# Two attention-plus-FFN layers on one core: the last FFN weights issued from ScalarE's queue instead of SyncE's

## The chip, the core and the metric

The kernel runs on one core of a Trainium2 chip. The metric is the device time of one execution in microseconds (us). The kernel before takes 2695.49 us, the median of three runs between 2694.4 and 2696.01 us. Lower is better.

## What is computed

The reference is two identical layers, each a recurrent attention followed by a gated feed-forward network (FFN). Cut to what matters:

```python
for s in range(n_seg):                      # 64 segments of 32 tokens, one after the other
    h = concat([mem, x[:, s*32:(s+1)*32]])  # 8 memory rows + 32 tokens
    q, k, v = h @ Wq, h @ Wk, h @ Wv        # 32 heads of 128, model width 576
    p = softmax(mask(q k^T * 128**-0.5))
    o = (p v) @ Wo
    mem = o[:, :8]                          # the next segment needs this segment's output
    outs.append(o[:, 8:])
x = x + outs(layernorm(x))
x = x + (silu(layernorm(x) @ w1) * (layernorm(x) @ w3)) @ w2     # FFN width 4608
# the same two lines once more (the second layer, same weights)
```

The memory rows make the segments a chain: segment s+1 cannot start before segment s has its output. The FFN has no such chain.

## The kernel before

**Steps and jobs.** Both layers run interleaved. `step(t)` does segment t of layer 0 and segment t - 8 of layer 1 together, so that there are 72 steps; the last eight serve layer 1 alone. After every fourth step comes `job(j)`, the FFN for a block of 128 tokens of each layer. An FFN job runs over 18 slices of 256 of the 4608 columns; a slice needs the tile `W13` (slices of w1 and w3, 256 KB twice and 32 KB twice) and `W2C` (288 KB in all of w2, two slices to a "down" product). These tiles have two buffers each and are loaded again for each job. The last job has no steps left beside it.

**Weights that stay, and the tail loads.** Wq and Wk lie in the tile `W`, Wv in `WV`, Wo in `WO`, for the whole kernel. When the last step has read a part of Wq and Wk for the last time, those columns are free, and the last job's FFN weights are put there: `tail_load(i, what)` (L705) for i = 0 to 3. With `what` = 0 it loads w1 and w3 for four slices into 1024 columns of `W`, in four transfers of 1024, 1024, 128 and 128 KB; with `what` = 1 it loads w2 for the same slices into `WV`, in one transfer of 1152 KB. All eight calls make 20 transfers, 14.2 MB. The last two of the 18 slices are kept from the job before. L477 holds what a call waits for: part i of `W` waits for the last step's Q and K projections numbered 2i and 2i+1 of eight (QK and QKt in the code), the parts of `WV` for the last step's V product. In the profile `W13` and `W` both appear as `W`, since buffer numbers are left out; their transfers are told apart by size.

**The last step.** Its four groups of eight heads each go through: projections (`HT,W` products), their copies out of PSUM (`QKT`), scores (`QKT` products), exponential on ScalarE (`SME<-SME`, one for each group, so four), row sums and probabilities on VectorE (`STAT`, `PB`), a transpose (`ident,PB`), its copies (`PTS`), the product with V (`PTS,V`), its copies (`OT`), and the product with Wo (`OT,WO`). Pieces of the FFN job before stand between them as filler: `XTB,W` products, a tanh on ScalarE (`HTT<-bank`), two multiplications on VectorE, and the down product `W2C,HTT`. After the last step a layer norm follows, and then the last job's 18 slices.

**What sets the order.** The order of TensorE's work is a string written out by hand (`ORDER`, L199 to L222; Q and q are projections, S scores, T transpose, P product with V, O product with Wo, F and f FFN). `plan()` (L76) lays everything else around it: a greedy list scheduler over queues ACT (ScalarE), DVE (VectorE), POOL, DMA (the queue that SyncE issues) and SWD. It picks by estimated times (`dur`, `lat`) and due times (`prio`), and gives copies marked "AD" to ScalarE or VectorE, whichever is free first by its estimate. It also hands out the eight PSUM banks. The order that it finds on each engine is then fixed: instructions of one engine are emitted in that order. `Emitter.dma` (L599) issues a transfer from SyncE's queue, `Emitter.adma` (L602) from ScalarE's queue; the latter is used only four times in the kernel before, at the very start.

**Completion semaphores.** The framework below the kernel adds the waits. Transfers from both hardware queues share eight completion semaphores, handed out in turn, in the order in which the plan emits the transfers. So each of them waits, at its place in its engine's queue, for the transfer that used its semaphore before to land, in most places the one eight earlier.

Of the kernel before, what the change touches and what calls it, by code (L numbers as in the profile page):

```python
# [9 lines left out]
ACT = mybir.ActivationFunctionType  # L10
# [3 lines left out]
P = 128  # L14
R64 = 64
D = 576
# [159 lines left out]
def actc(*ns):  # L176

    return sum(max(0.067 + n * 0.000833, 0.19) for n in ns)


def dve(*ns):
    return sum(max(0.065 + n / 960.0, 0.19) for n in ns)
# [11 lines left out]
def ewh(*ns):  # L194
    return (actc(*ns), dveh(*ns))
# [36 lines left out]
def make_nodes(em, nseg, pools, o=Opt, dma_bw=230e3, load_bw=400e3):  # L232
# [4 lines left out]
    def node(*a, **k):  # L237
        n = Node(*a, **k)
        nodes.append(n)
        return n  # L240

    def banks(n=2):
        return [Slot("bank") for _ in range(n)]

    nst = nseg + LAG
    kb = lambda rows, cols: rows * cols * 2
# [9 lines left out]
    def load(name, nbytes, prio, fn, deps=()):  # L256
        return node("DMA", nbytes / load_bw, fn, deps=deps, prio=prio, name=name, lat=2.0)
# [8 lines left out]
    b = banks(1)  # L266
# [10 lines left out]
    def ln_nodes(tag, src, xn, deps, prio, writes, warm=False):  # L277

        a = node("DVE", 1.16, em.ln_stats(src, xn), deps=deps, prio=prio, acq=[] if src is xn else [xn], name=tag + "stats")
        p_ = node("POOL", 0.45, em.ln_pow(xn), deps=[a], prio=prio, name=tag + "pow")  # L280
        c = node("DVE", 0.46 if src is xn else 0.66, em.ln_norm(src, xn), deps=[p_], prio=prio, name=tag + "norm")
        b = Slot("bank", users=len(writes))
        d = node("PE", 5 * 0.056, em.ln_tr(xn, b, warm), deps=[c], prio=prio, mode="full/col", acq=[b], rel=[xn], name=tag + "tr")
        out = []
        for wr, cost, more in writes:
            out.append(node("AD", cost, wr(b), deps=[d] + more + out[-1:], prio=prio, rel=[b], name=tag + "wr"))
        return out
# [12 lines left out]
    def ht_set(li, g, nodes_):  # L300
        i = -1
        for j in range(4):
            t = 4 * g + j + LAG * li
            i += j == 0 or role(t) == 0
            ht_ready[li, t] = nodes_[i]
# [136 lines left out]
    def post(li, g):  # L442

        b = banks(1)
        prio = 4 * g + 4 + LAG * li
        d = node("PE", 5 * 0.056, em.post_tr(li, g, b[0]), deps=[d for j in range(4) for d in yx[li, 4 * g + j]] + ([xr_ld[g]] if li == 0 else []),
                 prio=prio, mode="full/col", acq=b, name="POST")
        return node("DVE", dve(576), em.post_add(li, g, xr[g], b[0]), deps=[d], prio=prio, rel=b, name="POSTa")
# [5 lines left out]
    def job(j):  # L454

        ents = [(0, j)] if 0 <= j < ngrp else []
        if 0 <= j - 2 < ngrp:
            ents.append((1, j - 2))
        if not ents:
            return  # L460
        s0 = 4 * j + 4 if j < ngrp else 4 * j - 4 + LAG
        ne = len(ents)
        last = s0 >= nst
        wr = []
        prev_ff = list(last_up)
        cost = ewh(640)
        for (bi, g) in reversed(ents):
            pa = post(bi, g)
            wr += ln_nodes("F", xr[g], Slot("xn"), [pa], s0, [((lambda bi: lambda b: em.xtb_write(bi, b))(bi), cost, prev_ff)], last)
        mm = (128 * ne / 2.4 + 2.5) / 1000  # L470
        w2_last = {}
        tail = None
        if last:
            v_done, qk_done = last_reads
            tail = []
            for i in range(4):
                parts = [(0, 9 * 1024, qk_done[4 * i:4 * i + 4]), (1, 8 * 576, v_done)]  # L477
                tail += [[load("tail", kb(128, c), s0 + o.tail_at + 0.01 * i, em.tail_load(i, what), deps=dep) for what, c, dep in parts]] * 2

        npp = NPR // 2  # L480
        for at, pp in enumerate([npp - 1] + list(range(npp - 1)) if last else range(npp)):
            mids, w2s, htts, lds = [], [], [], []
            stays = last and pp == npp - 1
            for pr_ in (2 * pp, 2 * pp + 1):
                prio = s0 + o.ff + (o.win if s0 + 4 < nst else o.last_win) * (2 * at + pr_ % 2) / NPR
                if stays:
                    w13, w2 = kept[pr_]
                    ld = []
                    w2s.append(w2)
                elif last:  # L490
                    w13 = w2 = None
                    ld = tail[pp]
                else:
                    keep = s0 < nst <= s0 + 4 and pp == npp - 1
                    w13, w2 = Slot("w13", users=2 + keep), Slot("w2", users=ne + keep)
                    kept[pr_] = w13, w2
                    ld = [node("DMA", kb(1152, 256) / dma_bw, em.load_w13(pr_, w13), prio=prio - 1, acq=[w13], lat=2.0, name="W13")]
                    lds.append(node("DMA", kb(256, 576) / dma_bw, em.load_w2(pr_, w2), prio=prio - 0.99, acq=[w2], lat=2.0, name="W2l"))
                    w2s.append(w2)
                b = banks()  # L500
                htt = Slot("htt", users=ne)
                rel13 = [w13] if w13 else []
                fm = node("PE", 16 * mm, em.ffn_up(ents, pr_, w13, b, last and not stays, False), deps=wr + ld, prio=prio, mode="full/col",
                          acq=b + [htt], rel=rel13, name="FF")
                ff = node("PE", 2 * mm, em.ffn_up(ents, pr_, w13, b, last and not stays, True), deps=wr + ld, prio=prio + o.fft, mode="row",
                          acq=b + [htt], rel=rel13, name="FFt")
                a = node("ACT", actc(256 * ne), em.ffn_tanh(ents, b, htt), deps=[fm, ff], prio=prio - 0.5, name="tanh")
                c = node("DVE", 2 * dve(256 * ne) + 0.13, em.ffn_mul(ents, b, htt), deps=[a], prio=prio - 0.5, rel=b, name="mul")
                last_up[:] = [fm, ff]
                mids.append(c)  # L510
                htts.append(htt)
            for (bi, g) in ents:
                b = banks()
                d = node("PE", 8 * 0.1225, em.ffn_down(bi, pp, htts, w2s, b, last and not stays), deps=mids + lds, prio=prio + o.w2,
                         mode="full/col", acq=b, rel=htts + w2s, name="W2b" if bi else "W2")
                es = [node("DVE", dve(288), em.ffn_add(g, h, xr[g], b[h]), deps=[d], prio=prio + o.w2, rel=[b[h]], name="W2a")
                      for h in (0, 1)]
                w2_last[bi] = es
        for (bi, g) in ents:
            if bi == 0:  # L520
                ht_set(1, g, ln_nodes("L1", xr[g], Slot("xn"), w2_last[0], s0 + LAG - 4.2, ht_writes(1, g)))
            else:
                xn = Slot("xn")
                c = node("ACT", actc(576), em.fin_cast(xr[g], xn), deps=w2_last[1], prio=s0 + LAG - 4.2, acq=[xn], rel=[xr[g]], name="fin")
                node("SWD", 1.0, em.store(g, xn, last), deps=[c], prio=s0 + LAG - 4.2, rel=[xn], lat=3.0, name="store")
# [42 lines left out]
class Emitter:  # L568
# [136 lines left out]
    def tail_load(self, i, what):  # L705

        def f(n):
            T = self.T
            fa = i * 1024
            t13, t2 = T.W[:, :, fa:fa + 1024], T.WV[:, i * 8 * D:(i + 1) * 8 * D].rearrange("p (b d) -> p b d", b=8)  # L710
            if what != 1:
                for kind, wd in ((0, self.a.w1), (1, self.a.w3)):
                    self.dma(t13[:, 4 * kind:4 * kind + 4], wd[0:4 * P, fa:fa + 1024].rearrange("(c p) f -> p c f", p=P))
                for kind, wd in ((0, self.a.w1), (1, self.a.w3)):
                    self.dma(t13[kind * R64:(kind + 1) * R64, 8], wd[4 * P:D, fa:fa + 1024])
            if what != 0:
                self.dma(t2, self.a.w2[fa:fa + 1024, :].rearrange("(b p) d -> p b d", p=P))
            for h in range(4):
                self.tail_w[4 * i + h] = (t13[:, :, h * 2 * P:(h + 1) * 2 * P], t2[:, 2 * h:2 * h + 2])
        return f  # L720
# [607 lines left out]
```

## Time and profile before

| | before |
|---|---|
| time, median of 3 | 2695.49 us |
| span of the profiled run | 2694.7 us |
| PE busy | 2622.5 us (97%) |
| PEld (weight loads) busy | 2286.7 us (85%) |
| DVE busy | 2103.0 us (78%) |
| ACT busy | 1361.9 us (51%) |
| data moved | 322.08 MB, mean 120 GB/s |
| start of the last step's first projection | 2621.18 us |
| last tail transfer issued | 2673.23 us |

The table is from the page and the timeline. Over the whole span TensorE is nearly always busy, but the change concerns only the end: the last step starts at 2621 us, and everything that the change moves happens after it. So the views to read are those of the last 75 us: what each engine did there in order of time, what the SyncE queue waited for, and what the DMA engines moved. Busy time does not count DMA-issuing instructions; they stand in the timeline as SPq or ACTq.

### The profile page before, as it was taken

How to read it: one execution, taken by the hardware profiler on the slowest of the kernel's cores; microseconds unless marked ns; L12 is line 12 of the kernel's file. 1: busy time of each engine (PE TensorE's matmuls, PEld its weight loads, DVE VectorE, ACT ScalarE, POOL GpSimd, SP SyncE). 2: the span in 40 equal slices, each digit the busy share in tenths (PEclk: the TensorE clock that was granted, in tenths of full speed). 3: DMA queues.
4: the chain of work that ended last, by engine and by line, in shares of the span. 5: the costliest groups of instructions: out<-in, count | busy, mean ns of one | idle time of the engine just before them, and what ended most of it. 6: DMA issues, size and time to landing. Idle time of an engine off the chain costs nothing.

```text
span 2694.7 us, 137011 instructions
## 1 busy us (share of the span) xinstructions
PE 2622.5 (97%) x60931; PEld 2286.7 (85%) x60995; DVE 2103.0 (78%) x5463; ACT 1361.9 (51%) x3938; POOL 332.5 (12%) x400
## 2 busy tenths in 40 slices
PE   5999999999999999999999999999999999999998
PEld 4788888889888888888888888888888888888886
DVE  5777886887888788787878878787887878787876
ACT  2655554554545455454545445454545545454542
POOL 1111110110111011011101101010110101011110
PEclk8999999999999999999999999999999999999999
DMA  9064524343342334334233433423243442434457
GB/s 317 4 178 115 156 85 129 89 128 109 109 127 80 109 97 128 109 114 127 78 111 91 128 108 117 126 80 116 83 128 108 117 126 66 121 89 135 128 168 246
DMA packets 478178, 322.08 MB, mean 120 GB/s; under 512 B 26024, under 2 KB 467760, under 8 KB 476944
## 3 DMA queue, kind: packets, MB, share of 16 engines
q1 hardware_dynamic: 474048, 305.43, 38.4%
q8 instruction: 477, 7.82, 1.2%
q0 software_dynamic: 3024, 6.93, 0.9%
q10 hardware_dynamic: 512, 0.94, 0.2%
q14 instruction: 117, 0.96, 0.1%
HBM read 308.49 MB, written 2.36 MB: 115 GB/s over the span
## 4 chain that ended last, share of the span: by engine, by line
PE 85%; DVE 7%; DMA 3%; ACT 2%; issue 1%; SPq 1%; POOL 0%; ACTq 0%; DVEq 0%
PE bank L591 85%; DVE STAT L597 1%; ACT V L594 1%; DVE SME L597 1%; DVE HTT L597 1%; SPq L600 1%; DMA W<-in_B_w_dram 1%; DVE PB L597 1%; DMA W<-in_A_Wk_dram 1%; DVE V L597 1%; DVE XN L597 0%; DMA WO<-in_A_Wo_dram 0%; DVE LNS L597 0%; DMA XN<-in_A_x_dram 0%; ACT PTS L594 0%
## 5 line engine op out<-in xcount | busy, mean ns | idle before, releaser
L591 PEld LDWEIGHTS <-W 128*128 128x128 bf16 (+2 forms) x32176 | 1267.8, 100 | 130.0 <-issue 62.6
L591 PE MATMUL bank<-HT,W 128*128 128x80 bf16 (+3 forms) x23040 | 811.9, 197 | 21.6 <-issue 9.4
L591 PE MATMUL bank<-XTB,W 128*64 128x256 bf16 (+5 forms) x9136 | 659.3, 263 | 5.6 <-DMA W<-in_B_w_dram 3.7
L594 ACT ACTIVATE QKT<-bank 128x64 bf16<-128x64 f32 (+2 forms) x1500 | 349.7, 312 | 352.7 <-PE bank L591 347.1
L1006 POOL MEMSET PB<- 128x1024 bf16 x288 | 274.1, 952 | 1831.6 <-PE bank L591 1532.6
L591 PE MATMUL bank<-OT,WO 128*128 128x80 bf16 (+3 forms) x11520 | 407.0, 198 | 3.8 <-ACT OT L594 1.3
L591 PEld LDWEIGHTS <-WO 128*128 128x128 bf16 (+1 forms) x11520 | 379.9, 102 | 21.2 <-issue 9.0
L594 ACT ACTIVATE V<-bank 64x512 bf16<-64x512 f32 (+1 forms) x606 | 343.0, 585 | 94.7 <-PE bank L591 86.1
L591 PE MATMUL bank<-WV,HT 128*32 128x512 bf16 (+4 forms) x3520 | 364.5, 382 | 6.6 <-issue 3.8
L591 PE MATMUL bank<-W2C,HTT 128*64 128x288 bf16 (+1 forms) x3072 | 323.6, 287 | 1.4 <-DMA W2C<-in_B_w_dram 1.0
L597 DVE TENSOR_REDUCE STAT<-SME 104x8 f32<-104x320 f32 (+1 forms) x576 | 274.2, 476 | 11.4 <-ACT SME L594 6.1
L594 ACT ACTIVATE HTT<-bank 128x512 bf16<-128x512 f32 (+1 forms) x324 | 176.6, 553 | 208.5 <-PE bank L591 207.5
L597 DVE TENSOR_TENSOR PB<-SME,STAT 40x128 bf16<-40x128 f32 (+4 forms) x912 | 275.0, 336 | 8.5 <-DVE STAT L597 0.5
L597 DVE SCALAR_TENSOR_TENSOR XR<-bank,XR 128x288 f32<-128x288 f32 x576 | 245.9, 446 | 25.0 <-PE bank L591 20.8
L591 PEld LDWEIGHTS <-HT 128*32 128x32 bf16 (+5 forms) x3584 | 154.2, 98 | 124.8 <-issue 17.4
L597 DVE SCALAR_TENSOR_TENSOR HTT<-HTT,bank 128x512 bf16<-128x512 bf16 (+1 forms) x324 | 201.8, 623 | 74.2 <-ACT HTT L594 69.9
L591 PEld LDWEIGHTS <-HTT 128*64 128x64 bf16 (+1 forms) x3136 | 223.7, 105 | 35.7 <-issue 2.4
L594 ACT ACTIVATE OT<-bank 128x320 bf16<-128x320 f32 (+1 forms) x420 | 155.2, 403 | 147.6 <-PE bank L591 144.6
L597 DVE TENSOR_TENSOR HTT<-HTT,bank 128x512 bf16<-128x512 bf16 (+1 forms) x324 | 203.6, 629 | 27.7 <-DVE HTT L597 0.5
L594 ACT ACTIVATE SME<-SME 104x320 f32<-104x320 f32 (+1 forms) x288 | 135.2, 470 | 166.8 <-DVE SME L597 165.1
L597 DVE CAST QKT<-bank 128x128 bf16<-128x128 f32 (+4 forms) x548 | 147.6, 316 | 87.9 <-PE bank L591 85.6
L594 ACT ACTIVATE PTS<-bank 128x320 bf16<-128x320 f32 (+1 forms) x383 | 143.9, 403 | 131.6 <-PE bank L591 118.4
(61 smaller groups left out, 1831.3 us busy)
## 6 DMA issues: line engine op xcount, KB each, us to landing
W<-in_B_w_dram SPq DMA_DIRECT2D x612, 256.0 KB, 3.5
W2C<-in_B_w_dram SPq DMA_DIRECT2D x306, 288.0 KB, 3.2
W<-in_B_w_dram SPq DMA_DIRECT2D x612, 32.0 KB, 3.2
W<-in_B_w_dram SPq DMA_DIRECT2D x8, 1024.0 KB, 12.3
W<-in_A_Wq_dram SPq DMA_DIRECT2D x9, 512.0 KB, 9.7
WO<-in_A_Wo_dram SPq DMA_DIRECT2D x4, 1152.0 KB, 16.8
XR<-in_A_x_dram POOLq DMA_DIRECT2D x16, 288.0 KB, 3.6
WV<-in_B_w_dram SPq DMA_DIRECT2D x4, 1152.0 KB, 10.9
```

What stands on the lines that cost most here:

```text
L591: self.ch("PE", self.nc.tensor.matmul(out, lhsT=lhsT, rhs=rhs, start=start, stop=stop, skip_group_check=True, **k))
L594: self.ch("ACT", self.nc.scalar.activation(*a, **k))
L597: self.ch("DVE", getattr(self.nc.vector, fn_)(*a, **k))
L600: self.ch("SP", self.nc.sync.dma_start(out=out, in_=in_))
L1006: return lambda n: self.ch("POOL", self.nc.gpsimd.memset(self.T.PB[:, pb.i], 0.0))
```

## The change

The eight nodes of `tail_load` become nodes of the planner's ACT queue in place of its DMA queue, with an estimated cost of 2.0 us (w1 and w3) or 0.5 us (w2) on ScalarE and a latency of 2 us plus the transfer, and their transfers are issued with `adma` in place of `dma`. It is meant to let them start as soon as their columns are free: on SyncE's queue they stand in line with the `W13` and `W2C` loads, which wait for their buffers.

```diff
                 parts = [(0, 9 * 1024, qk_done[4 * i:4 * i + 4]), (1, 8 * 576, v_done)]
-                tail += [[load("tail", kb(128, c), s0 + o.tail_at + 0.01 * i, em.tail_load(i, what), deps=dep) for what, c, dep in parts]] * 2
+                tail += [[node("ACT", 0.5 * (4 - 3 * what), em.tail_load(i, what), prio=s0 + o.tail_at + 0.01 * i, deps=dep, name="tail", lat=2.0 + kb(128, c) / load_bw) for what, c, dep in parts]] * 2
...
                 for kind, wd in ((0, self.a.w1), (1, self.a.w3)):
-                    self.dma(t13[:, 4 * kind:4 * kind + 4], wd[0:4 * P, fa:fa + 1024].rearrange("(c p) f -> p c f", p=P))
+                    self.adma(t13[:, 4 * kind:4 * kind + 4], wd[0:4 * P, fa:fa + 1024].rearrange("(c p) f -> p c f", p=P))
                 for kind, wd in ((0, self.a.w1), (1, self.a.w3)):
-                    self.dma(t13[kind * R64:(kind + 1) * R64, 8], wd[4 * P:D, fa:fa + 1024])
+                    self.adma(t13[kind * R64:(kind + 1) * R64, 8], wd[4 * P:D, fa:fa + 1024])
             if what != 0:
-                self.dma(t2, self.a.w2[fa:fa + 1024, :].rearrange("(b p) d -> p b d", p=P))
+                self.adma(t2, self.a.w2[fa:fa + 1024, :].rearrange("(b p) d -> p b d", p=P))
```

Since the planner decides from its estimates, the order of other work moves as well. On TensorE it does not: both programs have the same products in the same order, with other PSUM banks in the last step. On SyncE the `W13` and `W2C` loads close ranks. On ScalarE the 20 transfers now stand between the activations of the last step; the order from the built program, the transfers of one call together:

```
HTT, QKT
W part 0 (4 transfers)
SME (exponential of group 0)
W part 1 (4)
HTT (tanh of a filler slice)
WV parts 0 to 3 (4)
SME (group 1)
W part 2 (4)
V, QKT, V x2, QKT x2
W part 3 (4)
SME (group 2), OT x2, SME (group 3), HTT, PTS x2, ...
```

and thirteen PSUM copies of the last step (six `QKT`, four `PTS`, two `V`, one `OT`) go from ScalarE to VectorE.

## Prediction

> **What bounds the kernel now.** I read the page first, for where the span goes. TensorE is busy in 97% of it, and the chain that ended last is TensorE for 85%. A change that touches only what happens after 2621 us can't move that bulk, so I went on to the last 75 us, by stretch, in the view of windows (columns after the stretch: length, busy time with count of PE, PEld, DVE, ACT, POOL, then granted clock, DMA share, GB/s):
>
> ```profile
> 2621.00:2631.00 10.00, 9.69 (x274) 7.80 (x273) 8.04 (x24) 3.65 (x13) 0.06 (x1) 1.00 0.91 303
> 2631.00:2641.00 10.00, 6.40 (x178) 5.88 (x178) 5.29 (x14) 5.48 (x17) 1.68 (x2) 0.79 1.01 286
> 2641.00:2651.00 10.00, 9.71 (x317) 9.30 (x315) 5.87 (x18) 3.86 (x14) 2.06 (x3) 0.87 0.51 151
> 2651.00:2661.00 10.00, 8.14 (x116) 6.44 (x111) 7.15 (x18) 1.28 (x4) 0.55 (x1) 1.00 1.07 354
> 2661.00:2671.00 10.00, 10.00 (x154) 8.73 (x152) 7.51 (x18) 2.85 (x7) 0.58 (x1) 1.00 1.07 364
> 2671.00:2683.00 12.00, 9.28 (x139) 7.72 (x138) 7.51 (x18) 2.30 (x6) 0.00 (x0) 1.00 0.83 280
> ```
>
> The reader is to see the DMA column: full from 2621 to 2641, half empty from 2641 to 2651, full again until 2680. TensorE is nearly full all the while. So the tail loads lose about 10 us to the SyncE queue, and the question is what that costs TensorE. The SyncE queue's timeline says where it stood (start, duration, what):
>
> ```profile
> 2634.88 0.45 SPq L600 DMA_DIRECT2D WV<-in_B_w_dram  x1
> 2643.86 2.14 SPq L600 DMA_DIRECT2D W<-in_B_w_dram  x3
> ```
>
> From 2635.3 to 2643.86 nothing is issued: the next W13 load waits for TensorE to leave its buffer, and 15 of the 20 tail transfers stand behind it. The waits of the SyncE queue between 2620 and 2675 agree:
>
> ```profile
> SPq L600 <- PE bank L591: 17.0, 10, 8.7
> SPq L600 <- DMA W<-in_B_w_dram: 1.7, 1, 1.7
> ```
>
> The second line is small, and matters most below: a transfer of SyncE's queue waited 1.7 us for an earlier transfer to land (its completion semaphore). The price that TensorE pays is in its timeline:
>
> ```profile
> 2658.61 0.40 PE L591 MATMUL bank<-W2C,HTT 128*128 128x288 bf16 x2 [0.58 <-DMA W2C<-in_B_w_dram]
> 2659.44 0.90 PE L591 MATMUL bank<-W2C,HTT 128*128 128x288 bf16 x6 [0.43 <-DMA W2C<-in_B_w_dram]
> ...
> 2672.63 0.23 PE L591 MATMUL bank<-XTB,W 64*128 64x128 bf16 x1 [0.69 <-DMA W<-in_B_w_dram]
> 2673.09 3.07 PE L591 MATMUL bank<-XTB,W 64*128 64x128 bf16 x51 [0.23 <-DMA W<-in_B_w_dram]
> ...
> 2682.47 0.84 PE L591 MATMUL bank<-XTB,W 128*128 128x128 bf16 x12 [1.80 <-DMA W<-in_B_w_dram]
> ```
>
> In brackets is what TensorE waited: 0.58 + 0.43 + 0.69 + 0.23 + 1.80 = 3.73 us. That is all that earlier tail loads can win, since nothing else between 2651 and the end waits for a transfer.
>
> ScalarE's side is its timeline around the third and fourth exponential of the last step:
>
> ```profile
> 2640.64 0.47 ACT L594 ACTIVATE SME<-SME 40x320 f32<-40x320 f32 x1
> 2642.51 0.50 ACT L594 ACTIVATE OT<-bank 128x160 bf16<-128x160 f32 x2 [1.40 <-PE bank L591]
> 2642.94 0.47 ACT L594 ACTIVATE SME<-SME 40x320 f32<-40x320 f32 x1
> ```
>
> **What the Trainium skill says.** "DMA: Bandwidth & Descriptors", Issuing engines are not separate DMA queues: transfers of all issuing engines run on the same 16 DMA engines and interleave; another issuer only saves issue time. So the 14.2 MB move no faster from ScalarE. No run shows that yet for this end. "Perfetto Trace Analysis", Per-instruction lifecycle: the sequencer of the issuing engine itself waits for a transfer's semaphores, then generates descriptors, and only then fetches the next instruction; ScalarE and VectorE are strictly first in, first out. The trace agrees for SyncE (the 1.7 us above, and 8.7 us behind TensorE). So on ScalarE a tail transfer that waits holds every activation behind it. "TensorE: Matmul & The Clock Gate", The HAM clock gate: after some 3.4 us of idleness TensorE runs at half clock until it has been busy as long. The trace shows less idleness suffice: the clock mean is 0.79 in 2631 to 2641, after a gap of 2.33 us.
>
> **The change part by part.** Removed: 20 transfers from SyncE's queue. SyncE waits for other things anyway; worth at most the 3.73 us above. Moved to VectorE: thirteen copies of 0.30 to 0.68 us, some 5 us. VectorE is busy 5.29 and 5.87 of 10 us in that stretch, and ScalarE loses as many, so I cost them at nothing.
>
> Added: 20 issues on ScalarE. An issue to an empty ring took 0.5 to 0.6 us on SyncE, so 20 x 0.55 = 11 us of ScalarE's time. That alone would be bearable, with ScalarE idle for half of the stretch.
>
> Added as well, and decisive: their waits. The built program names them. W part 0's third transfer waits until its first has landed; part 1's second for part 0's second; WV 2 and 3 for part 0's third and fourth; part 2's four for part 1's four; part 3's first two for WV 0 and 1, its third for part 2's first, its fourth for part 2's third. Behind each on ScalarE stand activations that TensorE needs, and nearest to the end is this: **the third exponential stands behind part 3, so it can't start before part 2's third transfer has landed.** TensorE's third transpose and all that follows in the hand-written order wait for it.
>
> When does that land? The rates are those of before. Landing times of its transfers, from issue and time to landing in the DMA view: the first 1 MB W transfer landed at 2629.6 and the second released SyncE at 2634.2 (that is the 1.7 us wait), 4.5 us later. In the full stretch after 2650, successive landings lie 3.0 us apart for a WV transfer (2662.4, 2665.4), 3.1 and 3.4 us for the two large transfers of a W part (2668.5, 2671.9), and some 1.1 us for its two small ones. A pair of W2C took 1.7 us, a set of W13 1.8 us. After the change, from 2629.5 for the very first (its columns come free at the same time as before, as TensorE's order hasn't changed):
>
> - rest of part 0: 4.0 + 0.6; part 1: 7.7; four WV: 12.0; part 2 up to its third: 7.1. Sum 31.4 us.
> - SyncE's own loads in between, one W2C pair and one W13 set: 1.7 + 1.8 = 3.5 us.
>
> Together 34.9 us, so 2664.4 us. With part 3's last issue of 0.6 us the third exponential starts at about 2665.0, against 2640.64 before: 24.4 us later. Earlier holds (the first tanh behind part 1 at some 2637 against 2627.87, the second exponential behind WV) lie inside this one.
>
> From there to the end TensorE's work is the same. Two corrections. Before, TensorE was the limit in the step's last groups: the third transpose came 4.06 us after the exponential (2644.70), though its probabilities were ready 2.74 us after it (2643.38). Now TensorE waits, so that this slack goes: minus 1.3 at that transpose. At the fourth it is less, as a restart at half clock costs 0.3 or more; I take minus 1.0 in all. The 3.73 us of waits vanish: part 3 lands at about 2671, and the last FFN, which used the tail from some 2662 on, now starts 23 us later. W2C is no longer queued behind WV.
>
> Sum: 2695.5 + 24.4 - 1.0 - 3.7 = 2715.2 us.
>
> Bounds: the largest unknown is the rate of the DMA engines. At the WV rate throughout (1.18 MB in 3.0 us, 393 GB/s) the 11.8 MB between the first landing and the deciding one take 30.0 us, so 2659.5, and the end is 2710.3. At what the whole stretch of 2645.5 to 2682.6 moved (11.95 MB in 37.1 us, 322 GB/s) they take 36.6 us and the end is 2716.9. A pause in TensorE's issue like the 2.33 and 1.17 us ones at 2631 and 2638 (marked as waiting for nothing shown, while the DMA was full) would add up to 3.5 us: 2720.
>
> **The rivals.**
>
> *Early loads win (faster).* If activations don't stand still behind a waiting transfer, the tail loads start some 10 us earlier and the 3.73 us vanish: 2695.5 - 3.7 = 2691.8. For it speaks the half-empty DMA of 2641 to 2651, and that ScalarE is only half busy. Against it, the order on ScalarE and the semaphores, both of the built program, and that SyncE does stand still in the same position.
>
> *A shorter hold (slower, by less).* If the transfers go at the best pace seen, 1.18 MB in 2.82 us (WV, the landing at 2675.9 after 2673.0), the deciding one lands at 2657.7, the end is at 2708.6; if TensorE packs the last groups 2.4 us tighter still, 2706. For it: one queue no longer starves, and two rings are fed. Against it: 354 to 364 GB/s was all that the full stretches moved.
>
> *A draw.* Delay and gain cancel only if the hold is 4.7 us, that is, if the third exponential started at 2645. By then about half of the bytes ahead of it would have landed. I see nothing for it.
>
> **How the numbers follow.** The long hold 0.73 (2710 to 2720, likeliest 2715.2), the shorter hold 0.12 (2701 to 2710), early loads 0.11, a draw 0.04. The two slower cases carry 0.85. The range of 2701 to 2721 leaves out the two other cases, 0.15, and the ends of the slow ones. Faster 0.11, same 0.04, slower 0.85.
>
> **What would show it.** In the changed profile: ACTq issues of the tail from about 2623.5 on, the last one only at about 2664; DMA full from 2626 to some 2671 with no half-empty stretch; the first tanh after the tail's start at about 2637, the third exponential at about 2665; gaps of several us on TensorE between 2630 and 2665, ended by ScalarE or VectorE; granted clock below 0.9 there; no wait for a transfer in the last FFN, and some 50 us from the third exponential to the end. The prediction is wrong if activations appear between the issues while a transfer waits, if the deciding transfer lands much before 2658, or if TensorE's gaps end up elsewhere than before that exponential.

## The result and the profile after

| | before | after |
|---|---|---|
| time, median of 4 | 2695.75 us | 2715.35 us |
| lowest to highest | 2694.4 to 2699.8 us | 2712.92 to 2720.05 us |
| span of the profiled run | 2694.7 us | 2718.3 us |
| first projection of the last step | 2621.18 us | 2622.66 us |
| third exponential of the last step | 2640.64 us | 2668.64 us |
| from there to the end | 54.06 us | 49.66 us |
| last tail transfer issued | 2673.23 us | 2668.10 us |

The changed kernel is slower: the ratio to before is 1.0072, with an interval of 1.0055 to 1.009. In the profiled run the last step begins 1.48 us later than before, so times of this trace are compared with those of before after taking 1.48 off.

The windows of the changed kernel, with the same columns as before (stretch, length, busy time and count of PE, PEld, DVE, ACT, POOL, then granted clock, DMA share, GB/s):

```profile
2621.00:2631.00 10.00, 8.51 (x273) 7.68 (x271) 5.34 (x17) 1.25 (x5) 0.00 (x0) 1.00 0.89 266
2631.00:2641.00 10.00, 3.44 (x36) 1.47 (x39) 2.69 (x9) 0.85 (x2) 0.00 (x0) 0.61 1.03 304
2641.00:2651.00 10.00, 4.67 (x136) 3.83 (x129) 4.14 (x10) 0.00 (x0) 0.95 (x1) 0.67 1.07 350
2651.00:2661.00 10.00, 1.29 (x31) 1.17 (x31) 3.79 (x10) 2.48 (x5) 0.00 (x0) 0.50 1.08 392
2661.00:2671.00 10.00, 5.98 (x131) 5.35 (x127) 4.16 (x13) 1.64 (x7) 0.95 (x1) 0.67 1.07 336
```

The DMA engines are now full without a break to 2671, as the change wanted, and TensorE pays: between 2631 and 2671 it is busy for 3.44 + 4.67 + 1.29 + 5.98 = 15.4 of 40 us. ScalarE computes for 5 us in that stretch. Its timeline shows what it did instead (start, duration, what, and in brackets the idle time before):

```profile
2624.96 10.59 ACTq L603 DMA_DIRECT2D W<-in_B_w_dram  x4
2635.60 0.47 ACT L594 ACTIVATE SME<-SME 40x320 f32<-40x320 f32 x1 [11.15 <-DMA W<-in_B_w_dram]
2636.74 3.12 ACTq L603 DMA_DIRECT2D W<-in_B_w_dram  x4
2639.91 0.38 ACT L594 ACTIVATE HTT<-bank 128x256 bf16<-128x256 f32 x1 [3.84 <-PE bank L591]
2639.99 12.32 ACTq L603 DMA_DIRECT2D WV<-in_B_w_dram  x4
2652.35 0.47 ACT L594 ACTIVATE SME<-SME 40x320 f32<-40x320 f32 x1 [12.06 <-DMA WV<-in_B_w_dram]
2652.43 6.46 ACTq L603 DMA_DIRECT2D W<-in_B_w_dram  x4
2658.94 0.59 ACT L594 ACTIVATE V<-bank 32x512 bf16<-32x512 f32 x1 [6.12 <-issue]
...
2661.37 7.23 ACTq L603 DMA_DIRECT2D W<-in_B_w_dram  x4
2668.64 0.47 ACT L594 ACTIVATE SME<-SME 40x320 f32<-40x320 f32 x1 [7.07 <-DMA W<-in_B_w_dram]
```

Five groups of transfers take 10.59 + 3.12 + 12.32 + 6.46 + 7.23 = 39.7 us of ScalarE's queue, and three of the four exponentials start within 0.1 us of the end of a group. TensorE's timeline has the other end of it:

```profile
2637.05 0.19 PE L591 MATMUL bank<-QKT 128*40 128x40 bf16 x1 [6.84 <-DVE QKT L597]
...
2653.97 0.19 PE L591 MATMUL bank<-QKT 128*40 128x40 bf16 x1 [8.28 <-DVE OT L597]
2659.89 0.40 PE L591 MATMUL bank<-QKT 128*40 128x40 bf16 x7 [5.74 <-ACT QKT L594]
```

VectorE is named for two of these gaps, but it had waited for the exponentials itself: 7.57 us before its row sum of 2652.85, released by ACT SME. In the last FFN TensorE waits for no transfer any more. The chain that ended last, followed through the same stretch, goes over the issues themselves and one landing (ACTq is an issue, DMA the time from an issue to its landing):

```profile
2645.70 3.63 ACTq L603
...
2649.43 2.87 ACTq L603
...
2652.43 2.84 ACTq L603
...
2656.82 11.21 DMA W<-in_B_w_dram
...
2668.10 0.49 ACTq L603
...
2668.64 0.48 ACT SME L594
```

### The profile page after: what moved, and what is told of

Its sections match the earlier page's. It is cut to its first block, busy times and chain, and to the rows that moved or that the text cites. A ratio compares the mean times of both kernels' runs of the same rounds, so it can differ in the third digit from the quotient of the medians.

```text
span 2718.3 us, 137019 instructions
## 1 busy us (share of the span) xinstructions
PE 2626.9 (97%) x60931; PEld 2288.6 (84%) x60995; DVE 2106.6 (77%) x5476; ACT 1358.0 (50%) x3925; POOL 332.3 (12%) x400
## 3 DMA queue, kind: packets, MB, share of 16 engines
q8 instruction: 477, 7.82, 1.2%
## 4 chain that ended last, share of the span: by engine, by line
PE 85%; DVE 6%; DMA 3%; ACT 3%; issue 1%; SPq 1%; ACTq 0%; POOL 0%; DVEq 0%
PE bank L591 85%; DMA W<-in_B_w_dram 1%; DVE STAT L597 1%; ACT V L594 1%; DVE HTT L597 1%; DVE PB L597 1%; DVE SME L597 1%; DMA W<-in_A_Wk_dram 1%; DVE V L597 1%; SPq L600 1%; ACTq L603 0%; DMA WO<-in_A_Wo_dram 0%; DVE XN L597 0%; DVE LNS L597 0%; DMA XN<-in_A_x_dram 0%
## 6 DMA issues: line engine op xcount, KB each, us to landing
WV<-in_B_w_dram ACTq DMA_DIRECT2D x4, 1152.0 KB, 14.2
```

## The experiments

My theory, T: activations stand behind tail transfers on ScalarE, for as long as the DMA engines need for the bytes ahead. Rivals: R1, the planner's new order costs the time (thirteen copies more on VectorE); R2, the bare issue time of 20 transfers on ScalarE. Ratios are to the kernel before, measured beside each kernel, with a 95% interval.

### The new order alone, and the new queue alone

The first kernel keeps the changed kernel's order on TensorE, VectorE and ScalarE, but its transfers go out from SyncE:

```diff
+                slots = [node("ACT", 0.5 * (4 - 3 * what), lambda n: None, prio=..., deps=dep, name="slot", lat=2.0) for what, c, dep in parts]
                 tail += [[load("tail", ...) for what, c, dep in parts]] * 2
```

> The changed kernel's order on TensorE, VectorE and ScalarE (thirteen copies moved to VectorE, other banks), but with the 20 tail transfers issued from SyncE as before: the planner keeps empty ScalarE slots where the changed kernel has its issues. Theory T (activations stand behind transfers that wait for landings): the reordering costs nothing, 2695.7 us give or take 2, no wait of TensorE above 3 us before the third exponential, which starts within 1 us of before. Rival R1 (the order that the planner made, with its thirteen copies on VectorE, is what costs): at least 2705 us.

Measured: 2692.71 us beside 2693.5 us for the kernel before, ratio 0.9994 (0.9985 to 1.0002). R1 falls as the cause of the loss: with the same order the queue makes the difference of 1.0072 - 0.9994 = 0.0078, or 21 us. The order is not free all the same. TensorE's timeline of this kernel:

```profile
2631.77 2.22 PE L591 MATMUL bank<-HT,W 128*128 128x40 bf16 x70 [1.75 <-issue]
...
2636.66 0.42 PE L591 MATMUL bank<-QKT 128*40 128x40 bf16 x7 [0.73 <-ACT QKT L594]
...
2640.52 0.40 PE L591 MATMUL bank<-QKT 128*40 128x40 bf16 x7 [1.48 <-DVE QKT L597]
```

It waits for copies that it did not wait for before; the third exponential comes 20.91 us after the first projection, against 19.46, so 1.45 us later and not within 1 us. In exchange the 3.73 us of waits for weights are gone here too. The planner's order changes the places of the loads on SyncE as well.

The second kernel keeps the order of the kernel before on every engine and changes only the queue:

```diff
-                    self.dma(t13[...], ...)
+                    self.adma(t13[...], ...)
```

> The order of the kernel before on every engine, with only the queue of the 20 tail transfers changed to ScalarE. Here ScalarE has part 0 before the first exponential, part 1 between copies of the last groups, and parts 2 and 3 among the tanh operations of the last FFN. Theory T: the first exponential stands until part 0's first transfer has landed (2629.6) and two more are issued, so at about 2631 against 2626.2 (some 3 us for TensorE); four issues ahead of an OT copy cost about 2 us; parts 2 and 3, which took 8.1 and 9.9 us of issue and waiting on SyncE, now hold tanh operations, some 6 us each; less the 3.7 us of waits for weights: about 2709 us, between 2700 and 2716. Rival R1 (the planner's new order is what costs): no loss, 2692 to 2697 us.

Measured: 2698.15 us, ratio 1.0019 (1.0012 to 1.0026), some 5 us slower. The direction is T's, the size is not: I had expected some 14, and at least 2700 us. The hold of the first exponential is there:

```profile
2621.78 7.54 ACTq L603 DMA_DIRECT2D W<-in_B_w_dram  x4
2629.37 0.47 ACT L594 ACTIVATE SME<-SME 40x320 f32<-40x320 f32 x1 [7.45 <-DMA W2C<-in_B_w_dram]
```

It comes 10.86 us after the first projection, against 5.06 before. The bracket names something that I had left out: the last thing waited for is a landing of SyncE's `W2C`, because part 0's fourth transfer uses the semaphore of that load. But parts 1 and 2 take only 2.26 and 2.29 us in this place, and part 3 takes 5.97, not 6 and more each. And the pauses of 2.33 and 1.17 us that TensorE had in the kernel before, ahead of the third exponential, are not there (others of 1.21 and 1.46 us come later). So it matters where the order puts the transfers: here only part 0 and one of WV stand ahead of the third exponential, in the changed kernel all 20.

### Part 3 out of the way

```diff
+def reordered(order): ...          # puts the last "tail" node behind the last "YTS"
-    for n in plan(nodes, pools, ORDER):
+    for n in reordered(plan(nodes, pools, ORDER)):
```

> The changed kernel with one edit: the four issues of W part 3 are moved on ScalarE from ahead of the third exponential to just behind the YTS copy of the last step. All other orders and the number of issues stay. Theory T: the third exponential then waits only for VectorE, whose subtraction ended at 2662.97 in the changed kernel's profile, so it starts at about 2663.0 instead of 2668.64, 5.6 us earlier, and the end follows: 2709.7 us, between 2707 and 2711. R1 (the order made by the planner) and R2 (the issue time of 20 transfers): no change, 2715.3 give or take 1.5.

Measured: 2716.64 us, ratio 1.0082 (1.0067 to 1.0097); no gain. In the trace the first half of the expectation holds: the third exponential comes 38.54 us after the first projection instead of 45.98. Then the gain is lost. TensorE and the chain of this kernel:

```profile
2681.94 0.41 PE L591 MATMUL bank<-W2C,HTT 128*128 128x288 bf16 x2 [2.50 <-DMA W2C<-in_B_w_dram]
2683.69 1.60 PE L591 MATMUL bank<-W2C,HTT 128*128 128x288 bf16 x6 [1.34 <-DMA W2C<-in_B_w_dram]
```
```profile
2673.72 9.93 DMA W2C<-in_B_w_dram
```

The last W2C pair is issued by SyncE 2 us after part 3's first transfer on ScalarE, and lands after 9.93 us: it shares the DMA engines with the 2.4 MB of part 3, the last of which lands only 0.2 us before it. TensorE waits 3.84 us and runs at half clock for 3.4 us afterwards, and from the third exponential to the end it now takes 56.46 us instead of 49.66. A transfer on another queue is not out of the way. So part 3 was moved once more, behind the first tanh after YTS, where W2C has been issued:

```diff
+    y = next(i for i in range(y, len(order)) if order[i].name == "tanh")     # in reordered(); y was the last "YTS"
```

> The changed kernel with the four issues of W part 3 moved on ScalarE behind the first tanh that follows the YTS copy, so behind the issue of SyncE's last W2C pair as well. In the run with part 3 right behind YTS the third exponential came 7.4 us earlier and YTS 6.4 us earlier than in the changed kernel, but W2C, queued behind part 3, landed only 10 us after its issue: waits of 2.50 and 1.34 us and then some 10 us at a lower clock. Theory T: with W2C ahead in the queues those waits go and the gain of 6.4 us stays: 2709 us, between 2707 and 2711. Rivals R1 and R2 (order, issue time): 2715 give or take 2.

Measured: 2710.91 us, ratio 1.0056 (1.0041 to 1.0071), against 1.0072 of the changed kernel: 4.3 us come back by the ratios, whose intervals overlap, and the stretch from the first projection to the end shrinks from 95.64 to 88.85 us in the traces. Third exponential after 38.77 us, then 50.08 us to the end, no wait for W2C. T says 2709 and is met only just within its range of 2707 to 2711; R1 and R2, at 2713 us or more, are not. But 38.77 is still 19 us above before: part 3 was only the last of the holds, and those of part 0, WV and part 2 remain.

### The same issues with an eighth of the bytes

Three kernels move 1.8 MB instead of 14.2 MB in the same 20 transfers; most of the last FFN's weights are left out. They differ in order and queue: the kernel before, the changed kernel, and the changed kernel's order from SyncE.

```diff
-    (t13[:, 4 * kind:4 * kind + 4], wd[0:4 * P, fa:fa + 1024]...)      (t2, w2[fa:fa + 1024, :]...)
+    (t13[:, 4 * kind, 0:512], wd[0:P, fa:fa + 512])                    (t2[:, 0], w2[fa:fa + P, :])
```

> The kernel before with its 20 tail transfers cut to about an eighth of their bytes (1.7 MB instead of 14.2 MB), so most of the last FFN's weights are left out and the columns keep their old contents; orders and number of issues stay, SyncE issues them. The control for the next kernel, and a test of the pauses of TensorE marked as issue (2.33 and 1.17 us in the kernel before; each ended 1.3 to 1.5 us after a 16 KB packet of the instruction queue had landed). Theory F (TensorE waits there for its own instructions, whose packets share the DMA engines with the tail): no pause above 0.4 us, no wait for weights, no half clock in 2631 to 2651 (that is 3.5 + 3.7 + about 2.5 us): about 2684 us, between 2682 and 2687. If the pauses are TensorE's own: about 2690 us.

> The changed kernel with its 20 tail transfers cut to about an eighth of their bytes, in the same way (most of the last weights left out); 20 issues on ScalarE, their order and their waits for landings stay, but what they wait for lands within some 2 us. Theory T (activations stand behind transfers that wait for landings): nearly all of the loss goes, 2 to 5 us above the control with the same cut, so 2685 to 2690 us; no wait of TensorE above 4 us. Rival R2 (the issue time itself, 20 times 0.4 to 0.55 us on ScalarE, and the reordering): 9 us or more above the control, 2693 us or more.

> The order of the changed kernel on TensorE, VectorE and ScalarE with the tail issued from SyncE, and the tail cut to an eighth of its bytes (most of the last weights left out), as in the two kernels with that cut. It splits the 6.6 us that the changed kernel with the cut (2690.75) lay above the kernel before with the cut (2684.18). In the run with the reordering alone TensorE waited 2.9 us for copies on VectorE and ScalarE (0.43, 0.30, 0.73, 1.48), which was hidden in the total as its 3.7 us of waits for weights had gone. Theory C (the thirteen copies on VectorE cost some 3 us, the issues on ScalarE the rest): about 2687.5 us, between 2686 and 2689. If the copies cost nothing, as predicted: 2684 give or take 1. If they are all of it: 2690.7.

| order, queue | ratio, all bytes | ratio, an eighth | first projection to third exponential, all / eighth |
|---|---|---|---|
| before, SyncE | 1 | 0.9955 (0.994 to 0.997) | 19.46 / 15.40 us |
| changed, SyncE | 0.9994 (0.9985 to 1.0002) | 0.9986 (0.9979 to 0.9993) | 20.91 / 19.08 us |
| changed, ScalarE | 1.0072 (1.0055 to 1.009) | 0.9983 (0.9975 to 0.9991) | 45.98 / 18.75 us |

The times are 2684.18, 2689.29 and 2690.75 us, beside 2694.81, 2693.2 and 2694.81 us for the kernel before. Three things follow.

First, T: with an eighth of the bytes the queue costs nothing (0.9983 against 0.9986), with all of them 0.0078. The issues are the same 20 in number and order, so R2 falls; the loss comes with the bytes. Against its own control the changed kernel with the cut lay 6.6 us higher, more than the 2 to 5 us that T allowed and less than R2's 9; the third kernel shows that this rest is the order's.

Second, part of my costing was wrong: the new order alone costs 0.9986 - 0.9955 = 0.0031, some 4 to 8 us, when nothing hides it (70.05 against 65.82 us from the first projection to the end in the traces, 8.4 us by the ratios). I had expected 3, and predicted nothing. TensorE's waits in the order-only kernel with the cut:

```profile
PE bank L591 <- DVE QKT L597: 1.9, 2, 1.5
PE bank L591 <- DVE OT L597: 0.7, 1, 0.7
PE bank L591 <- ACT QKT L594: 0.7, 1, 0.7
```

VectorE is busy for 9.23 of 10 us there (2626 to 2636), and TensorE's clock is halved for 10.2 us, against 3.4 us in the kernel before with the cut.

Third, the tail's bytes cost the kernel before 2694.81 - 2684.18 = 10.6 us, not just the 3.73 us of its waits for weights. From the first projection to the end the trace with the cut is 73.52 - 65.82 = 7.7 us shorter: 3.73 us of waits for weights, 2.2 us of pauses (3.50 to 1.30 us), and an estimated 1.7 us from half clock (half of the 3.4 us by which it shrinks, 6.8 to 3.4). The remaining 3 us lie ahead of the last step, where nothing was changed; the traces of this case reach that step anywhere between 2614.97 and 2622.66 us, so they are within what executions differ by. Not all of what was expected to go went: pauses of 0.45 and 0.85 us and 3.4 us of half clock are left.

### Earlier loads without ScalarE

Here the loads that held up SyncE's queue go to GpSimd's, and the tail stays on SyncE:

```diff
-        def f(n):
+        def f(n, dma=self.swdma if keep else self.dma):      # W13; W2C in the same way
```

> The kernel before with one other edit: the last step's W13 and W2C loads that wait for TensorE to leave their buffers (eight W13 transfers and two of W2C) are issued from GpSimd, so that the tail transfers behind them on SyncE needn't wait; ScalarE issues nothing. Theory T (tail loads started earlier do win the 3.73 us of waits if no activation stands behind them): 2691.8 us, DMA without a half-empty stretch from 2641 to 2651, no wait for a transfer in the last FFN. Rival R3 (with the DMA engines full, TensorE pauses more, as at 2631 and 2638): 2695 to 2698 us, pauses marked as issue above 3.5 us in sum.

Measured: 2699.3 us, ratio 1.0024 (1.0015 to 1.0032): slower, beyond what R3 said. The DMA engines are full from 2617 to 2667, no activation is held, and the last W transfers are long there when needed. TensorE's timeline:

```profile
2628.61 1.92 PE L591 MATMUL bank<-HT,W 128*128 128x40 bf16 x70 [1.52 <-issue]
...
2635.64 1.16 PE L591 MATMUL bank<-HT,W 128*128 128x40 bf16 x30 [3.36 <-issue]
...
2649.13 0.42 PE L591 MATMUL bank<-OT,WO 128*128 128x40 bf16 x7 [3.78 <-issue]
...
2663.39 0.41 PE L591 MATMUL bank<-W2C,HTT 128*128 128x288 bf16 x2 [2.23 <-DMA W2C<-in_B_w_dram]
2664.47 1.06 PE L591 MATMUL bank<-W2C,HTT 128*128 128x288 bf16 x6 [0.67 <-DMA W2C<-in_B_w_dram]
```

Pauses marked as issue have grown from 3.50 to 8.82 us, and half clock from 6.8 to 17.1 us. How much of the loss is due to GpSimd's queue itself, no run separates. What TensorE may be waiting for in the pauses stands on the page of every kernel of this case, among the DMA queues (packets, MB, share of the 16 engines):

```profile
q8 instruction: 477, 7.82, 1.2%
```

7.82 MB over 60,931 matmuls and 60,995 weight loads is 64 bytes each, in 477 packets of 16 KB, so 256 instructions to a packet. The Trainium skill ("Runtime: NRT & Kernel Launch", Instruction fetch mechanics) says just this: an engine's instruction memory is refilled in blocks of 16 KiB, or 256 instructions, over a DMA queue of its own, and crossing a block is "mostly hidden". At the end of this kernel it is not. The landings of these packets in the traces, beside the pauses:

| kernel | pause | TensorE goes on | last packet landed | later by |
|---|---|---|---|---|
| before | 2.33 us | 2633.21 | 2631.70 | 1.51 us |
| before | 1.17 us | 2638.88 | 2637.63 | 1.25 us |
| loads on GpSimd | 1.52 us | 2628.61 | 2627.16 | 1.45 us |
| loads on GpSimd | 3.36 us | 2635.64 | 2633.96 | 1.68 us |
| loads on GpSimd | 3.78 us | 2649.13 | 2647.69 | 1.44 us |
| new order, SyncE | 1.75 us | 2631.77 | 2630.31 | 1.46 us |
| before, an eighth | 0.85 us | 2640.60 | 2638.91 | 1.69 us |

And the first matmul after a pause of more than 0.2 us stands 2217, 1961, 1705, 1193 or 937 TensorE records before the end, its sequencer's records counted too, in whichever kernel: steps of 256, 256, 512 and 256. So the pauses are at the block boundaries, and wherever they occur in the last step they end 1.2 to 1.7 us after a block has come in. That a block waits for tail traffic is what the sizes suggest: the pauses of the last step sum to 3.5 us before, 2.4 in the new order from SyncE and 8.8 with the DMA engines full throughout, and to 1.3, 0.4 and 0 us in the three kernels with an eighth of the bytes. But the packets themselves take about 1 us in all of them, so the waiting would be ahead of the packet, and when each block was asked for, no record shows.

### Smaller pieces, a version better than both

```diff
-    self.dma(t13[:, 4 * kind:4 * kind + 4], wd[0:4 * P, fa:fa + 1024]...)
+    for c in range(4): self.dma(t13[:, 4 * kind + c], wd[c * P:(c + 1) * P, fa:fa + 1024])     # WV likewise, in four
```

> The kernel before with each large tail transfer (1024 and 1152 KB) cut into four, so that at most eight small ones (some 2.2 MB) can be in flight instead of eight large ones; same bytes, same queue, SyncE. A candidate for a version better than both. If the packets of instructions wait behind all that is queued (theory F with a deep queue), the pauses of 2.33 and 1.17 us shrink below 1 us in sum and the end is at about 2690 us. If the DMA engines serve the queues in turn, so that the depth is of no account, no change: 2693 give or take 2, or worse if the smaller transfers move fewer GB/s in the full stretches than the 354 to 364 of the kernel before.

Measured: 2692.14 us beside 2694.81, ratio 0.9988 (0.9979 to 0.9998). It has one pause,

```profile
2632.33 1.16 PE L591 MATMUL bank<-HT,W 128*128 128x40 bf16 x30 [1.71 <-issue]
```

instead of 3.50 us in two, and 4.2 us of waits for weights. So by the medians it lies ahead of both kernels, by 0.12% of the time before, but the interval ends only just short of 1. Whether a shorter queue is the reason is not shown: one trace with one pause less is thin, and the pauses did not shrink below 1 us as that reason had let me expect.

The same pieces with the changed kernel's order, from SyncE:

> A candidate for a version better than both: the order of the changed kernel on TensorE, VectorE and ScalarE, the tail issued from SyncE, and each large tail transfer cut into four. The run with this order alone had no wait for weights in the last FFN but pauses of 0.67 and 1.75 us and 2.9 us of waits for copies; the run with quarters alone had one pause of 1.71 us and still 4.2 us of waits for weights. If both gains add: no wait for weights above 0.5 us, pauses below 1.8 us in sum, 2689 to 2691 us where the kernel before has 2694. If the quarters bring back the waits for weights: 2692 to 2694.

Measured: 2691.45 us beside 2693.2, ratio 0.9995 (0.9984 to 1.0007). No wait for weights, one pause of 1.65 us, but 3.8 us of waits for copies. It can't be told from the kernel before, nor from either kernel that it combines; the question whether the gains add stays open.

## Why the prediction was right

The prediction was 2715.2 us and the result is 2715.35. Its cause is the one shown: the same 20 issues in the same order cost 21 us from ScalarE with all their bytes, and nothing with an eighth of them. By its steps, with times of the changed trace moved by the 1.48 us:

- **When the tail starts and how fast it lands.** First landing forecast at 2629.5, measured 2630.82 - 1.48 = 2629.3. The deciding transfer, part 2's third, forecast at 2664.4, measured 2668.03 - 1.48 = 2666.6. From part 1's last landing to this one it was 18.7 us against the 19.1 of the sum. The 2 us were lost earlier: parts 0 and 1 with SyncE's loads between them took 18.5 us after the first landing, not 4.6 + 7.7 + 3.5 = 15.8. The rate was not lower than in the sum (321 GB/s in this stretch); more bytes moved in it, 5.9 MB where the sum has 4.9, since transfers issued later took their share. From the first landing to the deciding one it was 12.9 MB, not 11.8, at 346 GB/s. The full stretch before (2650 to 2680) moved 358, so on the whole another queue was no faster.
- **The third exponential.** Forecast 24.4 us later than before, measured 26.5.
- **From there to the end.** Forecast 1.0 + 3.7 = 4.7 us shorter, measured 54.06 - 49.66 = 4.4. The 3.73 us are all gone, so 0.7 is left of the 1.0 (the clock stays halved for 6.8 us after the third exponential, against 3.0 before). With 26.5 - 4.4 = 22.1 and the 1.48 at the start, that is the 23.6 us between the two profiled runs. The changed kernel's was the longest of its measured times, 4.7 us above the median. So the agreement to 0.15 us is luck; the terms are good to some 2 us.
- **The issues.** "20 x 0.55 = 11 us" was mis-sized. The Trainium skill ("Perfetto Trace Analysis", Per-instruction lifecycle) puts the start of an issue in the profile behind its semaphore waits. Read so, the 20 single issues of the changed kernel last 24.3 us in all, WV's third 7.54 us alone, and waits account for the other 15 of the 39.7 us. With an eighth of the bytes the 20 issues last 9.8 us. Where much is queued, the issue itself is held; the kernel before had such issues on SyncE already, the longest of 4.53 us at 2655.07.
- **The waits.** Of those that I listed, part 0's and part 3's came true, 9.3 us by the trace's semaphore events, and the deciding one among them: part 3's fourth transfer is issued at 2668.10, 0.07 us after part 2's third landed. Those of WV and of part 2 were met before ScalarE came to them; there the issues were held. Another 5.0 us I had not listed: part 0's fourth and part 1's third and fourth transfer waited for `W2C` and `W13` of SyncE to land. The forecast survived because either brake lets go only as fast as bytes move, and bytes were what I had counted. No run takes the two brakes apart.
- **The copies, "costed at nothing".** Wrong by themselves, 4 to 8 us. In the changed kernel they should lie inside the hold, which no run shows by itself; with the tail on SyncE they are paid back by the waits for weights that go. The total didn't show the error.
- **The pauses.** I allowed up to 3.5 us more. It was one of 0.39 us: while TensorE stands for ScalarE, its instructions come in (blocks landed at 2632.75 and 2647.04, inside its gaps).
- **The rivals.** Early loads did remove all waits for weights, also where no activation was held (the new order from SyncE), but not to the gain of 3.7 us that I gave them: without any hold on ScalarE, a DMA kept full came with 6 us more, in the pauses, the waits for W2C and half clock. The short hold and the draw didn't come.
- **The signs.** First tanh behind part 1 forecast at 2637, measured 2638.4; last issue 2664 against 2666.6; DMA full to 2671, as forecast; TensorE's gaps at 2630 to 2659, ended by ScalarE and by VectorE behind it.

## What to carry to other kernels

A transfer moved to another engine's queue moves no bytes faster, and on an engine that computes it holds the work behind it as long as the bytes queued ahead need, those of another queue included where semaphores are shared: put large transfers there only where nothing urgent follows, and count bytes, not issues. Filling an empty stretch of the DMA engines isn't free either, since TensorE's instructions and other small loads share them; look for pauses marked as issue, at steps of 256 instructions. A term costed at nothing should be tried with the large effect taken away, or the total will hide it.

## What the runs showed that I had not expected

- TensorE's pauses marked as issue are waits for its own instructions: at block boundaries of 256, ended 1.2 to 1.7 us after the 16 KB packet landed, and up to 3.78 us long with full DMA engines.
- An issue of a transfer of 1.0 to 1.2 MB lasts from 0.37 to 7.54 us on ScalarE, with all its semaphores met. In the changed kernel the three longest end 0.04, 0.22 and 0.19 us after the landing of an older transfer of the same queue (part 1's last, WV's first and second), and in the two kernels with part 3 moved they end within 0.1 us of the same landings. So the queue seems to take only so much; how much, no run shows.
- Half clock needs no long idle stretch. In the changed order from SyncE with an eighth of the bytes the clock is halved from 2633.6 on, for 10.2 us. In the 3.4 us before, TensorE was busy for 67% and its longest single wait was 0.74 us. The Trainium skill ("TensorE: Matmul & The Clock Gate", The HAM clock gate) speaks of an idle window of some 3.4 us. No share of busy time explains all cases: in the kernel with quarters, a stretch of 3.4 us with 48% (2652.1 to 2655.5) was followed by the full clock. The way back is clearer: in the last step and the FFN of the twelve traces the full clock returned 22 times, always after 3.4 us in which TensorE was busy for 92% or more; in 32 other such stretches at half clock (counted off from the clock's changes) it was busy for 89% at most, and half clock stayed. The changed kernel, whose TensorE waits again and again, runs at half clock for 37.6 us there, the kernel before for 6.8.
